# Attention with scores made twice: maxima first, then keys by queries, with the division on the output

## The chip, the cores and the metric

The kernel runs on one core of one Trainium2 chip. A core has TensorE (PE, matmuls into PSUM; weight loads are shown as PEld), VectorE (DVE), ScalarE (ACT), GpSimd (POOL) and SyncE (SP, which here only issues DMAs). They run in parallel, each through its own instructions in order, and wait for one another by semaphores. PSUM is 8 banks of 2 KB per partition, a bank holding 512 float32 of each of 128 partitions. The metric is the device time of one execution in microseconds (us).

## The reference

Eight batches of 12 heads, 448 tokens and 64 elements per head go through attention, whose output is laid out as 768 features per token, and then through a gated MLP whose gate mixes tokens.

```python
q_n, k_n = rmsnorm(q, g_q), rmsnorm(k, g_k)       # over a head's 64 elements
scores = 1 / sqrt(64) * q_n @ k_n.T
attn = exp(scores - max(scores, axis=-1))
attn = attn / (sum(attn, axis=-1) + 1e-9)
x = (attn @ v) -> (batch, 448, 768)
h = gelu(x @ w_in)                                # 768 -> 1024, tanh form
u, v = h[..., :512], h[..., 512:]
v_n = (v - mean(v)) / sqrt(var(v) + 1e-6) * g_ln
v_s = w_sg @ v_n + b_sg                           # over the 448 tokens
out = x + (u * v_s) @ w_out
```

## The kernel before

Float32 values are carried as two float16 parts, high and low, and a product is made of two or three matmuls of such parts. Heads go in pairs (A, B): 48 pairs, six per batch. 448 tokens are three blocks of 128 and a tail of 64; a pair is seven columns of 128 rows, the tails of A and B sharing one.

Per pair `i` the work runs through these functions. `squares` and `norms` (lines 317 to 339) make the root mean squares of q and k, for two pairs at a time: a square on ACT, a sum on DVE, some ten short operations on DVE. `split` (line 341) multiplies by gains and norms on POOL, makes the high part on ACT and the low part on POOL, copies the keys' parts in swapped order on DVE, and turns all with one DMA transpose into `qt` (line 352). `vsplit` (line 377) makes the parts `vh` and `vl` of v.

`scores` (line 395) has a tile of 128 queries by 448 keys per step, seven per pair. Each is two matmuls that contract over 128 rows (a head's 64 elements, high and low; line 411), or, for the tile of the tails, two for each head on half of the output partitions. DVE takes the row maximum from PSUM (line 414), ACT the exponential with that as bias and with the row sums (line 416). For groups of two, two and three tiles DVE makes the reciprocal of the sums (lines 420 and 422). The weights are then scaled into a high part (on POOL for some tiles, line 430, on ACT for the others, line 432) and a low part (DVE, line 433). As queries lie on the partitions and `pv` needs keys there, DMA transposes on SP's queue (line 436, four per pair) turn both parts into `at`.

`pv` (line 442) has 11 steps per pair; in each, both heads' matmuls (384 and 64 columns, lines 453 and 455) write their half of the output partitions of one PSUM tile. ACT and DVE make the parts `xh` and `xl` of x (lines 461 and 462), which stay in SBUF.

`moe` (line 485) is the MLP of a batch: `mv` (line 517 and 520, v's half of `x @ w_in`), gelus in a `cluster` on ACT with a load of the gelu table before and of the exponential's table behind it (lines 471 and 480), the layer norm, `mu` (line 575, u's half), `ms` (line 605, mixing tokens; the last 64 tokens' contraction is on half of the rows), the gate, and `mo` (lines 639 to 651, the output with x added through an identity), whose outputs leave by ACT's DMA queue (lines 658 to 661).

Weights are read and decoded in the first pairs (`weights`, line 153). The order is set at three places. Line 709 loops over the pairs and, per pair, interleaves the steps of `scores(i)`, `pv(i - 1)`, the weights and the MLP of an earlier batch by their counts of steps; `low` (line 668) puts the MLP's instructions 200 places later in priority; and a planner lays every engine's instructions out by priority and by when it expects their operands. What it lays out is fixed: on the chip each engine goes through its list in order. PSUM: `ps_s` has four one-bank buffers for the scores, `ps_v` one for pv, `ps_m` three for everything of the MLP (lines 84 to 86).

Of the kernel before, what the change touches and what calls it, by code (L numbers as in the profile page):

```python
# [8 lines left out]
F32 = mybir.dt.float32  # L9
# [24 lines left out]
PT, PT0 = (0, 3, 6), (0, 2, 4, 6)
# buffers
NS, NV, NM = 4, 1, 3
NQK, NVR, GV, RAWB = 2, 2, 3, 3
NA, NAH, NAT, NQT, NVH, HLB = 4, 4, 2, 2, 2, 2
NOT, NX = 2, 12
BACC_KW = dict(dynamic_dma_scratch_size=1024)  # L40
# [4 lines left out]
def kernel(  # L45
# [16 lines left out]
    P = 128  # L62
# [11 lines left out]
    C7 = 2 * CM + 1  # L74
    EH = DM // 2
# [34 lines left out]
    def newton(y, x, t):  # L110
        """y, a guess of x ** -0.5 within 3.5%, made better by a step of third and one of second order."""
        V.tensor_tensor(out=t, in0=x, in1=y, op=ALU.mult)
        V.tensor_tensor(out=t, in0=t, in1=y, op=ALU.mult)
        V.scalar_tensor_tensor(out=t, in0=t, scalar=-10.0 / 3.0, in1=t, op0=ALU.add, op1=ALU.mult)
        V.scalar_tensor_tensor(out=y, in0=t, scalar=5.0, in1=y, op0=ALU.add, op1=ALU.mult)
        V.scalar_tensor_tensor(out=t, in0=x, scalar=-0.5 * 0.375 ** 3, in1=y, op0=ALU.mult, op1=ALU.mult)
# [36 lines left out]
    def weights():  # L153
        nonlocal mlp
        ctx_w = ExitStack()
        # w_in's parts take the place of its float32 values, one K block after the other
# [60 lines left out]
        for c in range(CK):  # L217
# [15 lines left out]
        for j in range(2 * FT):  # L233
# [25 lines left out]
    R = {}  # L259

    def load_qk(i, qs=None):
        if i >= NI:
            return
        qs = qs or [nc.scalar]
        nq = 0

        def put(out, in_):
            nonlocal nq
            qs[nq % len(qs)].dma_start(out=out, in_=in_)
            nq += 1  # L270

        b, g = divmod(i, NP)
        h0 = 2 * g
        qk = ld.tile([P, 2, 2 * C7, D], F32, name="qk", bufs=NQK)
        def mains(j):
            for x, src in enumerate((q, k)):
                d = qk[:, j, x * C7:(x + 1) * C7]
                put(bass.AP(tensor=d.tensor, offset=d.offset, ap=[list(d.ap[0]), [CK * D, 2], [1, CM * D]]),
                    src[b, h0 + 2 * j:h0 + 2 * j + 2, 0:SM].rearrange("h (p c) d -> p h (c d)", c=CM))
            R[i + j] = dict(qk=qk[:, j])  # L280

        mains(0)
        for x, src in enumerate((q, k)):
            for h in range(2):
                put(qk[h * HP:(h + 1) * HP, :, x * C7 + CM],
                    src[b, h0:h0 + 4, SM:S].rearrange("(j h) p d -> h p j d", h=2)[h])
        mains(1)
# [3 lines left out]
    def load_v(i):  # L291
        """A head's v in 7 columns: m0, m1, m2, (t, m0a), (m0b, m1a), (m1b, m2a), (m2b, t), with a and b
        the halves of a block: what meets the blocks of A's transposed weights and, from (t, m0a) on, of B's."""
        if i >= NI:
            return
        b, g = divmod(i, NP)
        vr = ld.tile([P, 2 * GV, C7, D], F32, name="vr", bufs=NVR)
        hs = slice(2 * g, 2 * (g + GV))
        mn = v[b, hs, 0:SM].rearrange("h (p c) d -> p h (c d)", c=CM)
        tl = v[b, hs, SM:S].rearrange("h p d -> p h d")  # L300
        lo, hi = vr[0:HP], vr[HP:P]
        for dst, src in ((vr[:, :, 0:3].rearrange("p h c d -> p h (c d)"), mn),
                         (hi[:, :, 3:6].rearrange("p h c d -> p h (c d)"), mn[0:HP]),
                         (lo[:, :, 4:7].rearrange("p h c d -> p h (c d)"), mn[HP:P]),
                         (lo[:, :, 3], tl),
                         (hi[:, :, 6], tl)):
            nc.sync.dma_start(out=dst, in_=src)
        for j in range(GV):
            VR[i + j] = vr[:, 2 * j:2 * j + 2].rearrange("p h c d -> p (h c d)")

    def v8(x):
        """Of a pair's columns A's 0..3 and B's 3..6."""
        return bass.AP(tensor=x.tensor, offset=x.offset, ap=[list(x.ap[0]), [10 * D, 2], [1, 4 * D]])
# [3 lines left out]
    def squares(i):  # L317
        gi, j = divmod(i, NG)
        if j == 0:
            SS[gi] = sml.tile([P, NG, SSW], F32, name="ss", bufs=2)  # L320
        qk = R[i]["qk"]
        sk = prep.tile([P, 896], F32, name="sqk", tag="t4", bufs=HLB)
        skv = sk[:, 0:SSW * D].rearrange("p (c d) -> p c d", d=D)
        A.activation(out=skv, in_=qk, func=AF.Square)  # L324
        V.tensor_reduce(out=SS[gi][:, j], in_=skv, axis=AX.X, op=ALU.add)  # L325

    def norms(i, cnt):
        gi, j = divmod(i, NG)
        n = cnt * SSW
        ss = SS[gi].rearrange("p a b -> p (a b)")[:, j * SSW:j * SSW + n]  # L330
        x, t = (sml.tile([P, NG * SSW], F32, name=f"n{c}", bufs=2)[:, 0:n] for c in "xt")
        si = sml.tile([P, NG * SSW], I32, name="ni", bufs=2)[:, 0:n]
        yt = sml.tile([P, NG * SSW], F32, name="ny", bufs=3)
        y = yf = yt[:, 0:n]
        V.tensor_scalar(out=x, in0=ss, scalar1=1.0 / D, scalar2=1e-6, op0=ALU.mult, op1=ALU.add)
        rsqrt_guess(yf, si, x)
        newton(yf, x, t)
        for j in range(cnt):
            R[i + j]["rs"] = y[:, j * SSW:(j + 1) * SSW]

    def split(i, E=G):
        r = R[i]
        qk = r["qk"]
        E.tensor_tensor(out=qk[:, C7:], in0=qk[:, C7:], in1=gg.unsqueeze(1).broadcast_to([P, C7, D]), op=ALU.mult)  # L344
        E.tensor_tensor(out=qk, in0=qk, in1=r["rs"].unsqueeze(2).broadcast_to([P, SSW, D]), op=ALU.mult)  # L345
        hl = prep.tile([P, 3 * C7, 2, D], F16, name="hl", tag="t4", bufs=HLB)
        A.activation(out=hl[:, 0:SSW, 0], in_=qk, func=AF.Copy)  # L347
        E.tensor_tensor(out=hl[:, 0:SSW, 1], in0=qk, in1=hl[:, 0:SSW, 0], op=ALU.subtract)  # L348
# [8 lines left out]
    def vsquares(i):  # L357
        """The sums of squares of the GV pairs of heads from i on."""
        if i >= NI:
            return  # L360
# [435 lines left out]
```

## Time and profile before

| | |
|---|---|
| median of 3 runs | 1049.37 us (1048.88 to 1051.4) |
| span of the profiled execution | 1047.2 us |
| its mean granted TensorE clock | 0.903 |
| busy: PE, DVE, ACT, POOL | 809.6, 899.9, 705.4, 504.6 us |
| DMA transposes of the weights | 192 |

The profiled execution was not timed apart from its profile, so its time is its span; the median of the runs is 2.2 us above it. Busy time is that of an engine's own work: waiting, and issuing DMAs, do not count. A matmul's recorded length has its passage through the array, so successive matmuls overlap in the record, and the distance between two starts is what one costs. In a row of a group, `x336 | 289.6, 886` means 336 instructions, 289.6 us busy in all, 886 ns as the mean of one; behind the second bar stands the engine's idle time just before them and what ended it.

### The profile page before, as it was taken

Reading aid. Unit: us, or ns where it says so; the run is one execution under the profiler, and the core shown is the slowest. Engines: PE = TensorE matmul, PEld = TensorE weight load, DVE = VectorE, ACT = ScalarE, POOL = GpSimd, SP = SyncE. Lnnn points to the kernel's source line nnn. Section 1 sums busy time; section 2 is a strip of 40 time slices with the busy share of each in tenths; the row PEclk is TensorE's granted clock in tenths of the full one; section 3 lists DMA queues with packets and bytes.
Section 4 is the critical chain, followed back from the end, with each engine's and each line's share of the span. In section 5 each row is a group of like instructions: output and inputs, shape, how many; then the busy total and the mean of one; then the engine's idle time right before and its main releaser. Section 6 shows DMA issues by size and latency. Waiting matters only on the chain. (4 is left out here: it accounts for less than half of the span.)

```text
span 1047.2 us, 17092 instructions
## 1 busy us (share of the span) xinstructions
PE 809.6 (77%) x5652; PEld 447.3 (43%) x5652; DVE 899.9 (86%) x1959; ACT 705.4 (67%) x1418; POOL 504.6 (48%) x435
## 2 busy tenths in 40 slices
PE   0333556757689798888979899887979799799998
PEld 0111222424454346444644357343634365346546
DVE  4999979999789997999979998999889988999430
ACT  2565787676677777677767767587667686877441
POOL 1777745637536463443545372545455443535021
PEclk9666688888899899899999899999989999999999
DMA  5969589685989979996797879994989779838501
GB/s 144 254 174 244 125 179 215 160 185 108 207 180 206 194 156 206 173 217 152 162 213 181 167 149 196 202 211 106 207 190 195 148 166 201 180 89 174 110 1 61
DMA packets 528217, 177.74 MB, mean 170 GB/s; under 512 B 472257, under 2 KB 521985, under 8 KB 528129
## 3 DMA queue, kind: packets, MB, share of 16 engines
q1 hardware_dynamic: 484928, 144.07, 66.6%
q10 hardware_dynamic: 43200, 32.59, 11.3%
q8 instruction: 44, 0.72, 0.3%
q14 instruction: 45, 0.36, 0.1%
HBM read 54.58 MB, written 11.01 MB: 63 GB/s over the span
## 5 line engine op out<-in xcount | busy, mean ns | idle before, releaser
L433 DVE SCALAR_TENSOR_TENSOR ahl<-a,rc,ahl 128x448 f16<-128x448 f32 x336 | 289.6, 886 | 32.1 <-POOL ahl L430 22.0
L416 ACT ACTIVATE a<-s,nm 128x448 f32<-128x448 f32 x336 | 211.0, 630 | 124.7 <-DVE ahl L433 78.0
L411 PE MATMUL s<-qt 128*128 128x448 f16 (+1 forms) x768 | 192.2, 388 | 120.8 <-ACT a L416 63.5
L430 POOL TENSOR_SCALAR ahl<-a,rc 128x448 f16<-128x448 f32 x150 | 117.3, 786 | 230.0 <-DVE rc L422 99.9
L414 DVE TENSOR_REDUCE nm<-s 128x1 f32<-128x448 f32 x336 | 200.2, 610 | 18.5 <-PE s L411 18.0
L432 ACT ACTIVATE ahl<-a,rc 128x448 f16<-128x448 f32 x186 | 118.1, 662 | 61.5 <-DVE rc L422 34.2
L411 PEld LDWEIGHTS <-qt 128*128 128x128 f16 (+1 forms) x768 | 57.2, 105 | 209.2 <-issue 127.8
L345 POOL TENSOR_TENSOR qk<-qk,ny 128x896 f32<-128x896 f32 x47 | 83.2, 1792 | 70.6 <-DVE ny L118 34.4
L348 POOL TENSOR_TENSOR hl<-qk,hl 128x896 f16<-128x896 f32 x47 | 95.7, 2037 | 34.4 <-ACT hl L347 26.3
L453 PE MATMUL pv<-at,vl 128*64 128x384 f16 x384 | 68.2, 368 | 56.7 <-DMA at<-ahl 44.8
L344 POOL TENSOR_TENSOR qk<-qk,gg 128x448 f32<-128x448 f32 x47 | 58.9, 1255 | 77.0 <-ACT sqk L324 76.8
L453 PE MATMUL pv<-at,vh 128*64 128x384 f16 x672 | 91.0, 357 | 0.0
L575 PEld LDWEIGHTS <-wi 128*128 128x128 f16 x576 | 57.4, 102 | 61.8 <-issue 15.9
L455 PE MATMUL pv<-at,vh 128*64 128x64 f16 x672 | 78.7, 202 | 0.0
L611 POOL TENSOR_TENSOR gt<-gt,u 128x448 f32<-128x448 f32 x32 | 39.0, 1221 | 79.0 <-DVE gt L610 59.2
L453 PEld LDWEIGHTS <-vl 128*64 128x64 f16 x384 | 30.7, 118 | 90.0 <-DMA at<-ahl 37.0
L416 ACT ACTIVATION_READ_ACCUMULATOR a<-s,nm 128x1 f32 x336 | 65.9, 196 | 0.0
L325 DVE TENSOR_REDUCE ss<-sqk 128x14 f32<-128x896 f32 x48 | 51.5, 1073 | 15.5 <-ACT sqk L324 15.2
L347 ACT ACTIVATE hl<-qk 128x896 f16<-128x896 f32 x48 | 45.3, 945 | 25.6 <-DMA qk<-in_k_dram 11.4
L324 ACT ACTIVATE sqk<-qk 128x896 f32<-128x896 f32 x48 | 45.3, 944 | 21.7 <-DVE ss L325 11.2
L453 PEld LDWEIGHTS <-vh 128*64 128x64 f16 x672 | 50.2, 120 | 18.6 <-issue 0.8
L420 DVE TENSOR_SCALAR rc<-sums 128x2 f32<-128x2 f32 x144 | 52.1, 364 | 7.1 <-ACT a L416 6.5
(995 smaller groups left out, 2096.0 us busy)
## 6 DMA issues: line engine op xcount, KB each, us to landing
qk<-in_k_dram ACTq DMA_DIRECT2D x48, 192.0 KB, 3.6
vr<-in_v_dram SPq DMA_DIRECT2D x16, 576.0 KB, 4.9
vr<-in_v_dram SPq DMA_DIRECT2D x32, 288.0 KB, 5.9
out_dram<-ot ACTq DMA_DIRECT2D x24, 384.0 KB, 3.8
qk<-in_q_dram ACTq DMA_DIRECT2D x46, 192.0 KB, 3.6
raw<-in_moe_w_in_dram SPq DMA_DIRECT2D x12, 512.0 KB, 4.9
vr<-in_v_dram SPq DMA_DIRECT2D x32, 96.0 KB, 4.9
at<-ahl SPq DMA_TRANSPOSE x192, 3.8
```

What stands on the lines that cost most here:

```text
L344: E.tensor_tensor(out=qk[:, C7:], in0=qk[:, C7:], in1=gg.unsqueeze(1).broadcast_to([P, C7, D]), op=ALU.mult)
L345: E.tensor_tensor(out=qk, in0=qk, in1=r["rs"].unsqueeze(2).broadcast_to([P, SSW, D]), op=ALU.mult)
L348: E.tensor_tensor(out=hl[:, 0:SSW, 1], in0=qk, in1=hl[:, 0:SSW, 0], op=ALU.subtract)
L411: mm(out=ps[p0:p1], lhsT=qt[:, t * P + p0:t * P + p1], rhs=qt[:, k0:k0 + S], start=(n == 0), stop=(n == 1))
L414: V.tensor_reduce(out=nm, in_=ps, axis=AX.X, op=ALU.max, negate=True)
L416: A.activation(out=a, in_=ps, func=AF.Exp, bias=nm, accum_out=sums[:, t - t0:t - t0 + 1])
L430: G.tensor_scalar(out=hl[:, 0], in0=a, scalar1=sc, scalar2=1.0, op0=ALU.mult, op1=ALU.mult)
L432: A.activation(out=hl[:, 0], in_=a, func=AF.Copy, scale=sc)
L433: V.scalar_tensor_tensor(out=hl[:, 1], in0=a, scalar=sc, in1=hl[:, 0], op0=ALU.mult, op1=ALU.subtract)
L453: mm(out=o[:, 0:SM].rearrange("p (c n) -> p c n", c=CM), lhsT=w, rhs=at[:, h * CK:h * CK + CM, blk], start=(n == 0), stop=(n == n_s - 1), ...
L455: mm(out=o[:, SM:S], lhsT=w, rhs=at[:, CM, blk, h * HP:(h + 1) * HP], start=False, stop=(n == n_s - 1), skip_group_check=True)
L575: done = mm(out=ps[:, 0:S], lhsT=ww[:, g, f * P:(f + 1) * P], rhs=xx, start=(n == 0), stop=(n == 17))
```

## The change

The scores are made twice and the weights come out with keys on the partitions, as `pv` needs them. `maxima(i)` multiplies the high parts alone, queries on the partitions, and takes each query's maximum. The negated maxima, as float16, are turned into a row (a matmul of the maxima against an identity) and copied to SBUF with ln 256 added; what is subtracted need not be the exact maximum, since the division takes it out again. `scores(i)` has keys on the partitions: three products of parts and a fourth that adds the row, then exponential, high part and low part. `pv(i)` first sums the weights over the keys by matmuls with ones, ACT makes the reciprocal as exp(-ln(sum)), one step of Newton corrects it, and the output is multiplied by it. The 192 transposes and `rc` are gone.

Each head keeps to one half of TensorE's rows: `qt` holds head A's 64 elements on partitions 0 to 63 and B's on 64 to 127, in four parts (q high, q low, k high, k low), for two pairs at a time, made by two transposes of 14 columns. PSUM is shared out anew: `ps_s` two buffers of two banks (for maxima, row and scores), `ps_v` one each for sums and pv, `ps_m` two. Token `7 p + c` now goes to block `c`, in 64 rows, so that loads, outputs, `w_sg` and `b_sg` are cut in seven; q and k are loaded on SP's queue, eight DMAs per two pairs, v once per batch without repeated columns, and outputs leave on SP's queue, two DMAs per tile. The MLP is as before, but at the two early batches two tiles of `mv` in place of three run along with the heads, and which results of `mv` and `mu` are copied out of PSUM ahead of their gelu is changed. The activation table set that holds exponential and logarithm is loaded in place of the exponential's.

```diff
-NS, NV, NM = 4, 1, 3
+SC, SR, SV = 4, 5, 5          # steps per pair: scores, maxima, pv
+EX = 256.0
+NS, NV, NM = 2, 1, 2
...
     def split(u, E=G):
+        qt = att.tile([P, 4, C7 * P], F16, name="qt", bufs=NQT)
+        for x in range(2):
+            qk = r["qk"][:, x].rearrange("p h c d -> p (h c) d")
+            if x:
+                E.tensor_tensor(out=qk, in0=qk, in1=gg..., op=ALU.mult)
+            E.tensor_tensor(out=qk, in0=qk, in1=r["rs"]..., op=ALU.mult)
+            A.activation(out=h_, in_=r["qk"][:, x], func=AF.Copy)
+            E.tensor_tensor(out=l_, in0=r["qk"][:, x], in1=h_, op=ALU.subtract)
+            r["tr"] = nc.sync.dma_start_transpose(out=qt[:, 2 * x:2 * x + 2]..., in_=hl...)
...
+    def bank(t, n, h):
+        return t[:, h, 0:S] if n == P else t[h * HP:(h + 1) * HP, 0, 0:S]
+
+    def maxima(i):
+        for c, (c0, n) in enumerate(tiles):
+            ps = ps_s.tile([P, 2, 512], F32, name="mx", tag="s")
+            for h in range(2):
+                hs = slice(h * HP, (h + 1) * HP)
+                mm(out=bank(ps, n, h), lhsT=qt[hs, 0, c0:c0 + n], rhs=qt[hs, 2, cols], start=True, stop=True)
+            V.tensor_reduce(out=nm[:, 2 * c:2 * c + 2], in_=ps[:, :, 0:S], axis=AX.X, op=ALU.max, negate=True)
+            yield
+        ps = ps_s.tile([P, 2, 512], F32, name="row", tag="s")
...
+                mm(out=ps[hs, 0, o:o + n], lhsT=nm[ks, x:x + 1].broadcast_to([n, HP]), rhs=ident_h[ks, ks], ...)
+        A.activation(out=row, in_=ps[:, 0, 0:S], func=AF.Copy, bias=LN_EX)
+
     def scores(i):
+        for c, (c0, n) in enumerate(tiles):
+            ps = ps_s.tile([P, 2, 512], F32, name="s", tag="s")
+            for m, (kx, qx) in enumerate(((2, 0), (2, 1), (3, 0), (None, None))):
+                for h in range(2):
+                    if m < 3:
+                        mm(out=bank(ps, n, h), lhsT=qt[hs, kx, c0:c0 + n], rhs=qt[hs, qx, cols], start=(m == 0), stop=False)
+                    else:
+                        mm(out=bank(ps, n, h), lhsT=part_h[hs, 0:n], rhs=row[hs], start=False, stop=True)
+            A.activation(out=p_, in_=p_, func=AF.Exp)
+            A.activation(out=h_, in_=p_, func=AF.Copy)
+            V.tensor_tensor(out=l_, in0=p_, in1=h_, op=ALU.subtract)
+            yield
-                nm = sml.tile([P, 1], F32, name="nm", bufs=6)
-                V.tensor_reduce(out=nm, in_=ps, axis=AX.X, op=ALU.max, negate=True)
-                A.activation(out=a, in_=ps, func=AF.Exp, bias=nm, accum_out=sums[:, t - t0:t - t0 + 1])
-            V.tensor_scalar(out=rc[:, 0:n], in0=sums[:, 0:n], scalar1=1.0 / ASC, scalar2=1e-9 / ASC, ...)
-            V.reciprocal(out=rc[:, 0:n], in_=rc[:, 0:n])
-                    G.tensor_scalar(out=hl[:, 0], in0=a, scalar1=sc, scalar2=1.0, op0=ALU.mult, op1=ALU.mult)
-                    A.activation(out=hl[:, 0], in_=a, func=AF.Copy, scale=sc)
-                V.scalar_tensor_tensor(out=hl[:, 1], in0=a, scalar=sc, in1=hl[:, 0], op0=ALU.mult, op1=ALU.subtract)
-                    nc.sync.dma_start_transpose(out=at[:, first:t + 1]..., in_=ahl[:, 0:cnt]...)
...
     def pv(i):
+        steps = [[(x, slice(0, P), c + h * C4, 2 * c + h) if c < CM else (x, slice(h * HP, (h + 1) * HP), CM, 2 * CM)
+                  for h in range(2)] for c in range(C4) for x in range(2)]
+        sm = ps_v.tile([P, 512], F32, name="sm")[:, 0:S]
+        for n, hx in enumerate(steps):
+            for h, (x, ks, _, t) in enumerate(hx):
+                mm(out=sm[h * HP:(h + 1) * HP], lhsT=one_h[ks], rhs=(ph, pl)[x][ks, t], ...)
+        A.activation(out=ln, in_=sm, func=AF.Ln)
+        A.activation(out=rc, in_=ln, func=AF.Exp, scale=-1.0)
+        ps = ps_v.tile([P, 512], F32, name="pv")[:, 0:S]
+        for vx, px in ((vh, ph), (vl, ph), (vh, pl)):
+            for hx in steps[::2]:
+                for h, (_, ks, c, t) in enumerate(hx):
+                    mm(out=ps[h * HP:(h + 1) * HP], lhsT=vx[ks, c], rhs=px[ks, t], ...)
+            yield
+        V.scalar_tensor_tensor(out=sm, in0=sm, scalar=1e-9 * EX, in1=rc, op0=ALU.add, op1=ALU.mult)
+        V.tensor_tensor(out=y, in0=ps, in1=rc, op=ALU.mult)
+        V.scalar_tensor_tensor(out=ps, in0=sm, scalar=-2.0, in1=y, op0=ALU.add, op1=ALU.mult)
...
-                nc.scalar.dma_start(out=om[t], in_=ot)
+            for h in range(2):
+                nc.sync.dma_start(out=om[1][t + h * C4] if t < CM else om[h][CM], in_=ot[h * HP:(h + 1) * HP])
...
         streams = []
         if i < NI:
-            streams.append((scores(i), 14))
+            streams.append((scores(i), SC))
+        if i + 1 < NI:
+            streams.append((maxima(i + 1), SR))
         if i > 0:
-            streams.append((pv(i - 1), 4))
+            streams.append((pv(i - 1), SV))
```

More of the change, by code (lines that the diff above doesn't have):

```diff
@@ L96 @@
     make_identity(nc, ident)
+    ident_h = const.tile([P, P], F16, name="ident_h")
+    A.activation(out=ident_h, in_=ident, func=AF.Copy)
+    one_h = const.tile([P, HP], F16, name="one_h")
+    V.tensor_copy(out=one_h, in_=ones[:, 0:HP])
+    part_h = const.tile([P, P], F16, name="part_h")
+    V.tensor_scalar(out=part_h, in0=ones, scalar1=1.0 / HP, scalar2=None, op0=ALU.mult)
     swap = const.tile([P, P], F32, name="swap")
@@ L263, in load_qk @@
+    lo, hi = slice(0, HP), slice(HP, P)
+    def load_qk(u, qs=None):
+        if u >= NI // NG:
             return
-        qs = qs or [nc.scalar]
+        qs = qs or [nc.sync]
         nq = 0
[L267 to L280, printed above, removed]
@@ L282, in load_qk @@
-        mains(0)
-        for x, src in enumerate((q, k)):
[L284 to L287, printed above, removed]
+        b, h0 = u // NU, u % NU * 2 * NG
+        qk = ld.tile([P, 2, 2, C7, D], F32, name="qk", bufs=NQK)
+        for x, src in enumerate((q, k)):
+            for half, j, b0, c0, n in ((lo, 0, 0, 0, C4), (hi, 0, 0, C4, CM), (lo, 1, C4, C4, CM), (hi, 1, CM, 0, C4)):
+                qs[nq % len(qs)].dma_start(
+                    out=qk[half, x, :, b0:b0 + n].rearrange("p h c d -> p h (c d)"),
+                    in_=src[b, h0 + 2 * j:h0 + 2 * j + 2].rearrange("h (p c) d -> p h (c d)", c=C7)[:, :, c0 * D:(c0 + n) * D])
+                nq += 1
@@ L289, with load_v @@
+        U[u] = dict(qk=qk)
     VR = {}
-    def load_v(i):
-        if i >= NI:
+    def load_v(b):
+        if b >= B:
             return
[L296 to L309, printed above, removed]
@@ new lines, in load_v @@
+        for j, h, half, s0, c0, n in ((0, 0, lo, 0, 0, C4), (0, 0, hi, 0, C4, CM), (0, 1, lo, C4, 0, CM), (0, 1, hi, CM, CM, C4),
+                                      (1, 0, lo, 0, C4, CM), (1, 0, lo, CM, 0, 1), (1, 0, hi, 0, 1, CM),
+                                      (1, 1, lo, C4, C4, CM), (1, 1, hi, CM, 0, C4)):
+            nc.sync.dma_start(out=vp[half, :, j, s0 * D:(s0 + n) * D], in_=src[j, h][:, :, c0 * D:(c0 + n) * D])
+        for g in range(NP):
+            VR[b * NP + g] = vr[:, g].rearrange("p c d -> p (c d)")
@@ L322, in squares @@
+    SS = {}
+    def squares(u, x):
+        if x == 0:
+            SS[u] = sml.tile([P, 2, SSW], F32, name="ss", bufs=2)
         sk = prep.tile([P, 896], F32, name="sqk", tag="t4", bufs=HLB)
         skv = sk[:, 0:SSW * D].rearrange("p (c d) -> p c d", d=D)
[L324 to L334, printed above, removed]
-        V.tensor_scalar(out=x, in0=ss, scalar1=1.0 / D, scalar2=1e-6, op0=ALU.mult, op1=ALU.add)
[L336 to L339, printed above, removed]
@@ new lines, in squares, with norms @@
+        V.tensor_reduce(out=SS[u][:, x], in_=skv, axis=AX.X, op=ALU.add)
+    def norms(u):
+        n = 2 * SSW
+        ss = SS[u].rearrange("p a b -> p (a b)")
+        x, t = (sml.tile([P, n], F32, name=f"n{c}", bufs=2) for c in "xt")
+        si = sml.tile([P, n], I32, name="ni", bufs=2)
+        y = sml.tile([P, n], F32, name="ny", bufs=3)
+        V.tensor_scalar(out=x, in0=ss, scalar1=1.0 / D, scalar2=1e-6, op0=ALU.mult, op1=ALU.add)
+        rsqrt_guess(y, si, x)
+        newton(y, x, t)
+        U[u]["rs"] = y
@@ new lines, in pv @@
+        ln, rc, y = (att.tile([P, S], F32, name=x, bufs=1) for x in ("ln", "rc", "y"))
+        A.activation(out=ln, in_=sm, func=AF.Ln)
+        A.activation(out=rc, in_=ln, func=AF.Exp, scale=-1.0)
+        yield
+        ps = ps_v.tile([P, 512], F32, name="pv")[:, 0:S]
+        n = 0
+        for vx, px in ((vh, ph), (vl, ph), (vh, pl)):
+            for hx in steps[::2]:
+                for h, (_, ks, c, t) in enumerate(hx):
+                    mm(out=ps[h * HP:(h + 1) * HP], lhsT=vx[ks, c], rhs=px[ks, t], start=(n == 0), stop=(n == 3 * C4 - 1),
+                       skip_group_check=True)
+                n += 1
+            yield
```

268 lines of the change are left out of this document (117 added, 151 removed).

## The prediction

> **What bounds the kernel now.** I read the page's busy line and slices first, then the table of stretches, then the groups of instructions kept apart by shape, then the timeline of TensorE. The page:
>
> ```profile
> span 1047.2 us, 17092 instructions
> PE 809.6 (77%) x5652; PEld 447.3 (43%) x5652; DVE 899.9 (86%) x1959; ACT 705.4 (67%) x1418; POOL 504.6 (48%) x435
> PEclk9666688888899899899999899999989999999999
> ```
>
> The stretches (span; PE, PEld, DVE, ACT, POOL busy with counts; granted clock, DMA share, GB/s) show a start, a long even middle and a drain. The second fence is the same view for line 461 alone (ACT's first output copy, one per pair of heads), so its count is the number of pairs finished; the third is line 411 (the scores' matmuls), the fourth the tile pv (PE, DVE, ACT).
>
> ```profile
> 0.00:250.00 250.00, 123.59 (x734) 56.30 (x734) 223.57 (x469) 158.58 (x311) 145.62 (x116) 0.77 0.78 179
> 250.00:985.00 735.00, 631.00 (x4552) 355.63 (x4553) 663.97 (x1455) 524.52 (x1074) 348.94 (x308) 0.94 0.84 179
> 985.00:1047.20 62.20, 55.02 (x369) 35.33 (x367) 12.34 (x36) 22.33 (x34) 10.07 (x12) 0.99 0.08 26
> ```
> ```profile
> 250.00:985.00 735.00, 21.33 (x40) 0.94 0.84 179
> ```
> ```profile
> 250.00:985.00 735.00, 148.38 (x614) 43.80 (x614) 0.94 0.84 179
> ```
> ```profile
> 250.00:985.00 735.00, 111.94 (x1720) 24.40 (x40) 21.33 (x40) 0.94 0.84 179
> ```
>
> In the middle 40 pairs take 735 us: 18.4 us per pair. DVE is busy 664.0/40 = 16.6 us of each (90%), PE 15.8, ACT 13.1. Of PE's 15.8, scores are 148.4/40 = 3.7, pv 2.8, and the MLP the remaining 9.3. In the start DVE is busy 89%. So **DVE sets the pace** in both, with PE at 86% behind it; only the drain is PE's. The question is whether PE has 2.6 us per pair to spare for what the change adds.
>
> **DVE, ACT, POOL and DMA, per pair** (group busy time over 48 pairs). What they spend now:
>
> ```profile
> L433 DVE SCALAR_TENSOR_TENSOR ahl<-a,rc,ahl 128x448 f16<-128x448 f32 x336 | 289.6, 886 | 32.1 <-POOL ahl L430 22.0 <-ACT ahl L432 10.1
> L416 ACT ACTIVATE a<-s,nm 128x448 f32<-128x448 f32 x336 | 211.0, 630 | 124.7 <-DVE ahl L433 78.0 <-DVE nm L414 32.4 <-DVE rc L420 4.1
> L414 DVE TENSOR_REDUCE nm<-s 128x1 f32<-128x448 f32 x336 | 200.2, 610 | 18.5 <-PE s L411 18.0
> L432 ACT ACTIVATE ahl<-a,rc 128x448 f16<-128x448 f32 x186 | 118.1, 662 | 61.5 <-DVE rc L422 34.2 <-issue 11.4 <-DVE nt L116 2.6
> L430 POOL TENSOR_SCALAR ahl<-a,rc 128x448 f16<-128x448 f32 x150 | 117.3, 786 | 230.0 <-DVE rc L422 99.9 <-ACT a L416 28.3 <-DVE rc L420 16.6
> L416 ACT ACTIVATION_READ_ACCUMULATOR a<-s,nm 128x1 f32 x336 | 65.9, 196 | 0.0
> L325 DVE TENSOR_REDUCE ss<-sqk 128x14 f32<-128x896 f32 x48 | 51.5, 1073 | 15.5 <-ACT sqk L324 15.2
> L384 ACT ACTIVATE vh<-vr,v_s 128x896 f16<-128x896 f32 x48 | 49.6, 1035 | 6.8 <-DVE v_s L134 3.8 <-DMA at<-ahl 2.9
> L386 DVE SCALAR_TENSOR_TENSOR vl<-vr,v_s,vh 128x512 f16<-128x512 f32 x48 | 47.3, 986 | 0.1
> L347 ACT ACTIVATE hl<-qk 128x896 f16<-128x896 f32 x48 | 45.3, 945 | 25.6 <-DMA qk<-in_k_dram 11.4 <-DVE ss L325 5.3 <-DMA qt<-hl 4.5
> L420 DVE TENSOR_SCALAR rc<-sums 128x2 f32<-128x2 f32 x96 | 32.5, 343 | 1.3 <-ACT a L416 1.1
> L462 DVE SCALAR_TENSOR_TENSOR xl<-pv,xh 128x448 f16<-128x448 f32 x48 | 29.3, 610 | 9.5 <-ACT xh L461 9.5
> L461 ACT ACTIVATE xh<-pv 128x448 f16<-128x448 f32 x48 | 25.6, 533 | 18.0 <-PE pv L455 17.7 <-PE s L411 0.2
> L351 DVE COPY hl<-hl 128x448 f16<-128x448 f16 x48 | 25.4, 531 | 0.1
> ```
>
> - DVE loses the low parts (289.6/48 = 6.03), the seven maxima (4.17), the row scales of the first two groups (0.68; the smaller reciprocals are left out) and a copy of key halves (0.53): 11.4 us, with the 0.99 of vl. It gets maxima on 896 wide tiles (3 at line 325's 1.07, also 896 wide, and one at 0.61: 3.8), low parts `l_` (3 + 1 of the same sizes; line 462, which reads PSUM and one SBUF tile likewise, took 0.61 for half: 3.8 to 4.3, I take 4.0), three operations of the division at 0.61 (1.8), and vl of 448 (0.99 x 448/512 = 0.87). That is 10.5 against 12.4: 1.9 off for certain; the reciprocals and the other copy add perhaps 1. I take **3 us** with them and without the slowing of line 433 (0.89 for what line 462 does in 0.61). DVE comes to 13.6 to 14.7 per pair.
> - ACT loses (211.0 + 65.9 + 118.1 + 49.6)/48 = 9.3 and gets exp and the high copy of 896 (6 at 0.945, from line 347) and of the tail (2 at 0.53, from line 461), the row 0.53, logarithm and exponential of the sums 2 x 0.63 (line 416), vh 0.53: 9.0. No change.
> - POOL loses 117.3/48 = 2.4 and is nowhere near the pace.
>
> ```profile
> at<-ahl SPq DMA_TRANSPOSE x192, 3.8
> qk<-in_k_dram ACTq DMA_DIRECT2D x48, 192.0 KB, 3.6
> ```
>
> - The 192 transposes of the weights leave SP's queue, and with them a landing of 3.8 us between scores and pv. The q, k loads (ACT's queue until now) and the outputs come to SP: 8 loads per two pairs, two outputs per MLP tile, 9 loads of v per batch. A load waits for its qk buffer, with the transposes of later keys behind it; it is issued two units (some 37 us) ahead, against a landing of 3.6. Cost nothing; if that cover were gone, 3.6 us in each of 24 units, 86 us.
>
> **TensorE.** Its timeline (start, length, instruction, count) gives the price of a matmul as the distance of starts:
>
> ```profile
> 600.23 0.35 PE L605 MATMUL ms__6887<-ws_l,vh 128*128 128x448 f16 x1
> 600.42 0.35 PE L605 MATMUL ms__6804<-ws_h,vl 128*128 128x448 f16 x1
> 600.71 0.36 PE L605 MATMUL ms__6804<-ws_h,vh 64*128 64x448 f16 x1
> ...
> 602.26 0.36 PE L605 MATMUL ms__6887<-ws_h,vh 64*128 64x448 f16 x1
> 602.26 0.36 PE L605 MATMUL ms__6804<-ws_h,vl 64*128 64x448 f16 x1
> 602.46 0.35 PE L605 MATMUL ms__6887<-ws_l,vh 64*128 64x448 f16 x1
> 602.47 0.35 PE L605 MATMUL ms__6832<-ws_h,vl 64*128 64x448 f16 x1
> ```
> ```profile
> 604.59 0.34 PE L453 MATMUL pv<-at,vh 128*64 128x384 f16 x2
> 604.75 0.20 PE L455 MATMUL pv<-at,vh 128*64 128x64 f16 x2
> 604.78 0.34 PE L453 MATMUL pv<-at,vh 128*64 128x384 f16 x2
> ```
>
> Three things are to be seen. A matmul of 448 columns takes 0.19 us of PE (600.23 to 600.42). Two on different halves of the rows start together (602.26 twice, 602.46 and 602.47), and so do two heads on halves of the columns (x2, with 0.19 from 604.59 to 604.78): a slot of 0.19 holds two heads. And when the shape of the array changes, the next start is 0.29 later, not 0.19 (600.42 to 600.71): **0.1 us per change of shape**.
>
> Slots per pair now: scores 6 tiles x 2 and the tail 2, 14; pv 11. 25 x 0.19 = 4.75 us (busy is 6.5: a lower clock, ends, changes of shape). After: maxima 4, scores 4 tiles x 4 (three products and the row), sums 8, pv 12: 40 x 0.19 = 7.6, and four short ones for the row, 128 columns, 4 x 0.19 x 128/448 = 0.2. So 7.8, and with the MLP's 9.3 **PE needs 17.1 us per pair before any change of shape**.
>
> Changes of shape: today full tiles of the scores have the MLP's shape, 128 by 128. After the change nothing of attention has: maxima and scores are 64 by 128, sums and pv 128 by 64, tails 64 by 64. Nine pieces per pair (4 maxima, row, 4 scores) take the two PSUM buffers one by one as these come free, between MLP matmuls: in and out, 18. The sums and pv run in 4 groups, each with a tail step, some 7 more. At least 12, if pieces stay together; at most 33, if each is alone. I take 25, nearer the upper end, because the buffers come free singly: 2.5 us (bounds 1.2 and 3.3). PE then needs 19.6 (18.3 to 20.4).
>
> How full PE can be is bounded by DVE's 90% in the middle and by this stretch, where PE has 53.97 of 60 (90%), at a full clock, just before the attention ends:
>
> ```profile
> 900.00:960.00 60.00, 53.97 (x381) 28.85 (x380) 57.44 (x126) 45.56 (x92) 30.84 (x28) 1.00 0.60 129
> ```
>
> A PE that sets the pace gets the full clock, which gives back up to 6% of its columns (0.94 in the middle) against these 90%; I take 96% net. 19.6/0.96 = 20.4 us per pair.
>
> **New waits.** The scores' fourth product needs the row, a copy on ACT behind the four maxima on DVE; the next pair's maxima run beside this pair's scores, so a pair's time (18 us) covers it, and only the first pair pays. The division hangs on sums, logarithm, exponential and three operations on DVE, with one PSUM buffer each for sums and pv: 1.5 + 2 x 0.63 + 3 x 0.61 + 0.53 + 0.61 = 5.7 us, within one pair's time too. PE's next sums wait behind it, and MLP matmuls behind these, only if it more than doubles. Nothing is added.
>
> **The sum.** Middle: 40 x (20.4 - 18.4) = +80. Start: 8 pairs in which DVE sets the pace and PE is busy 123.6 of 250: 3 us each, -24; the first keys and queries are now split for two pairs before any score, on DVE, three operations of 896 more at 1.07, +3: -21. Drain: with two PSUM buffers for the MLP in place of three, only two tiles of v are summed ahead; the third, 18 matmuls of 512 columns (0.19 x 512/448 = 0.22 each), moves behind the last head: +4, and 1 for waits: +5 (0 to 10). The profiled execution spans 1047.2 and the median of the runs is 1049.4, so 2.2 lie around it: 1047.2 + 80 - 21 + 5 + 2.2 = **1113**. PE from 18.3/0.98 = 18.7 to 20.4/0.90 = 22.7 gives 1045 to 1205; a start that gains 24 to 30, and the shapes below 12, reach lower.
>
> **Rivals.**
> - *Changes of shape are few, and it gets faster.* With 9 per pair (0.9 us) PE needs 18.0, at 98% 18.4: the middle keeps its time, and the start's gain stands: 1047.2 - 21 + 5 + 2.2 = 1033. Equality is at 18.8 us per pair, which at 98% is 13 changes of shape. For it: line 411's matmuls ran in fours between others. Against: only two PSUM buffers for nine pieces.
> - *The two PSUM buffers of the scores set the pace.* A full scores tile holds one through 4 slots of two matmuls' time (0.76), exp and copy (0.945 each) and the low part (1.07), 3.7 us; the tail 2.4, a maximum 1.3 (0.8 for the tail's), the row 0.8: 3 x 3.7 + 2.4 + 3 x 1.3 + 0.8 + 0.8 = 19.0 us, 9.5 per pair over two buffers. Every handing over, 17 of them, may meet another operation of up to 1 us on ACT or DVE. Half a wait of 1.5 us leaves it harmless, the whole 1.5 makes (19.0 + 25.5)/2 = 22.3: 1033 + 40 x 3.9 = 1189. For it, waits of this kind today, with four buffers (us, times, longest):
>
> ```profile
> ACT a L416 <- DVE ahl L433: 78.0, 80, 4.7
> PE s L411 <- ACT a L416: 63.5, 40, 7.9
> ```
>
> - *The tails of the two heads do not run together.* They lie in the two halves of one PSUM bank and on different halves of the rows, where the pairs at 602.26 wrote two tiles. Then the tails' 10 slots (maxima 1, scores 4, sums 2, pv 3) double: 1.9 us per pair, at 96% 2.0 x 40 = 80: 1193. The Trainium skill says of row halves that different row tiles cannot access the same PSUM bank at the same time (TensorEngine Tiling (Array Packing), Gotcha 1: PSUM Pressure); no run here shows such a pair yet. By that rule the time would be this rival's, by the row at 602.26 the forecast's.
> - *The halves don't overlap at all.* 20 more slots, 3.8 us, +158 at 96%: 1271. Against: the rows at 602.26.
>
> **Chances.** PE sets the pace at some 20.4 us: 0.46. Few changes of shape: 0.22. PSUM buffers: 0.15. Tails one after the other: 0.14. No overlap: 0.03. About 0.3% (3 us) is what can be told from no change. Within 3 us I count 0.03 of the first case (its fast edge) and 0.01 of the second: slower 0.43 + 0.15 + 0.14 + 0.03 = 0.75, no change 0.04, faster 0.21. The range, 1026 to 1190, leaves out the fastest of the second case, half of the two cases near 1190, and the last; the likeliest alone has 1075 to 1150 (19.4 to 21.3 us per pair).
>
> **What would show it.** After: DVE down to 75% or less of the middle with PE at 90% or more and the clock near 1.0; maxima and scores in pairs of equal start 0.19 apart; 0.1 more where shapes change. Tails: two starts together or 0.19 apart. Waits of PE for ACT or DVE at the scores above 2 us per pair would make it the buffers. A PE below 85% with less time would make the forecast wrong in kind, a middle below 18.8 us per pair in sign.

## The result and the profile after

The changed kernel takes 1292.96 us (median of 4 runs, 1291.99 to 1293.67) against 1050.38 us before on the same chip: a ratio of 1.2318, with a 95% interval of 1.226 to 1.2376. Slower was forecast, but 1113 us, and the time lies far above the range of 1026 to 1190. The profiled execution spans 1291.1 us. Below, a time without an interval behind its ratio is that of a single run.

The page of the changed kernel:

```profile
span 1291.1 us, 18006 instructions
PE 1056.3 (82%) x6996; PEld 479.4 (37%) x6996; DVE 781.4 (61%) x1430; ACT 727.3 (56%) x1095; POOL 347.7 (27%) x259
PEclk9666779999888997999888998999789899999899
```

The same stretches as before, cut where 7, 40 and 1 pairs of heads are finished, as they were there (columns: span; PE, PEld, DVE, ACT, POOL busy with counts; clock, DMA share, GB/s), and below it the count of the pairs, line 475 being ACT's first output copy:

```profile
0.00:260.00 260.00, 152.00 (x902) 57.59 (x904) 194.73 (x361) 156.74 (x243) 106.55 (x78) 0.79 0.40 104
260.00:1225.00 965.00, 849.90 (x5760) 387.10 (x5758) 574.25 (x1034) 548.28 (x818) 231.07 (x170) 0.93 0.23 52
1225.00:1291.10 66.10, 54.38 (x338) 34.66 (x338) 12.38 (x36) 22.32 (x34) 10.05 (x12) 0.97 0.10 25
```
```profile
0.00:260.00 260.00, 3.76 (x7) 0.79 0.40 104
260.00:1225.00 965.00, 21.71 (x40) 0.93 0.23 52
```

By this cut a pair takes 965/40 = 24.1 us in the middle, 18.4 before and 20.4 in the forecast. DVE has fallen to 14.4 us of it (60%), PE risen to 21.2 (88%). So PE is the busiest by far, and yet it stands still for 2.9 us per pair, and the clock is 0.93 and not full.

The cut at 260 us falls inside a long eighth pair, whose output copy starts at 278.6 us (at 250.4 before). Whole pairs compare better: from the eighth output copy to the 48th (1225.0 and 987.2 us) a pair takes 23.7 us, and 18.4 before. So the miss of 180 us is the middle's 40 x (23.7 - 20.4) = 130, and the start's 49: it takes 28 us more than before where 21 less were forecast. The drain behind the 48th copy (66 us against 60) is as forecast.

Who PE and the others waited for (us in all, times, longest):

```profile
PE s L431 <- DVE nm L401: 104.4, 42, 8.3
PE mx L399 <- DVE pl L438: 24.8, 18, 5.4
PE mx L399 <- DVE nm L401: 15.9, 8, 5.8
DVE pl L438 <- ACT ph L437: 142.5, 70, 5.6
DVE nm L401 <- PE mx L399: 127.5, 58, 4.3
DVE ss L316 <- ACT sqk L315: 60.3, 23, 5.7
ACT s L436 <- PE s L433: 159.2, 87, 5.8
ACT hl L341 <- DMA qt<-hl: 38.0, 15, 4.2
```

PE waits for DVE at maxima and scores (145 us in these three rows), DVE for ACT at the low parts, ACT for PE at the scores: a ring in which each stands idle for the next. What they share are the two PSUM buffers, which maxima and scores take in turn: line 431 does not read the maxima, so its wait for one is for the buffer that the maximum frees. One stretch shows a second thing in that ring (PE, DVE and ACT; start, length, and in brackets the idle time before):

```profile
497.83 0.68 PE L465 MATMUL pv<-pl,vh 128*64 128x448 f16 x3
502.11 0.55 PE L399 MATMUL mx<-qt 64*128 64x448 f16 x2 [3.60 <-DVE nm L401]
507.27 1.31 PE L431 MATMUL s<-qt 64*128 64x448 f16 x6 [4.61 <-DVE nm L401]
```
```profile
493.95 0.62 DVE L438 TENSOR_TENSOR pl<-s,ph 128x448 f16<-128x448 f32 x1 [0.45 <-ACT ph L437]
499.98 1.09 DVE L316 TENSOR_REDUCE ss<-sqk 128x14 f32<-128x896 f32 x1 [5.40 <-ACT sqk L315]
500.98 1.08 DVE L401 TENSOR_REDUCE nm<-mx 128x2 f16<-128x896 f32 x1
```
```profile
497.02 0.95 ACT L341 ACTIVATE hl<-qk 128x896 f16<-128x896 f32 x1 [2.38 <-DMA qt<-hl]
498.99 0.95 ACT L315 ACTIVATE sqk<-qk 128x896 f32<-128x896 f32 x1 [1.02 <-DMA qt<-hl]
```

ACT waits for a transpose of keys to give back a staging buffer, DVE's sum of squares waits 5.4 us for ACT, a maximum stands behind that sum in DVE's queue, and PE waits for the maximum. The ring and this chain are both waits for buffers. The theories, told in the expectations as they were formed before the runs: A, the keys' staging buffers; B, the scores' two PSUM buffers; C, PE's own work.

### The profile page after: what moved, and what is told of

Its sections match the earlier page's. It is cut to its first block, busy times and chain, and to the rows that moved or that the text cites. A ratio compares the mean times of both kernels' runs of the same rounds, so it can differ in the third digit from the quotient of the medians.

```text
span 1291.1 us, 18006 instructions
## 1 busy us (share of the span) xinstructions
PE 1056.3 (82%) x6996; PEld 479.4 (37%) x6996; DVE 781.4 (61%) x1430; ACT 727.3 (56%) x1095; POOL 347.7 (27%) x259
## 4 chain that ended last, share of the span: by engine, by line
PE 57%; DVE 17%; DMA 8%; ACT 7%; issue 5%; POOL 3%; SPq 2%; POOLq 0%; DVEq 0%; ACTq 0%
PE pv L465 7%; PE s L431 7%; PE sm L452 6%; DMA qt<-hl 5%; DVE nm L401 3%; DVE pl L438 3%; PE mx L399 2%; PE s L433 2%; DVE ss L316 2%; POOL qk L337 1%; SPq L285 1%; DVE sm L470 1%; DVE y L471 1%; ACT s L436 1%; ACT sqk L315 1%
## 5 line engine op out<-in xcount | busy, mean ns | idle before, releaser
L438 DVE TENSOR_TENSOR pl<-s,ph 128x896 f16<-128x896 f32 x192 | 186.2, 970 | 144.1 <-ACT ph L437 142.5
L431 PE MATMUL s<-qt 64*128 64x448 f16 (+1 forms) x1152 | 163.3, 388 | 113.6 <-DVE nm L401 104.4
L436 ACT ACTIVATE s<-s 128x896 f32<-128x896 f32 x192 | 155.5, 810 | 177.9 <-PE s L433 159.2
L401 DVE TENSOR_REDUCE nm<-mx 128x2 f16<-128x896 f32 x144 | 156.3, 1085 | 127.5 <-PE mx L399 127.5
L437 ACT ACTIVATE ph<-s 128x896 f16<-128x896 f32 x192 | 157.0, 819 | 2.6
L399 PE MATMUL mx<-qt 64*128 64x448 f16 (+1 forms) x384 | 78.2, 400 | 68.6 <-DVE pl L438 24.8
L431 PEld LDWEIGHTS <-qt 64*128 64x128 f16 (+1 forms) x1152 | 54.1, 101 | 194.2 <-issue 176.7
L452 PE MATMUL sm<-ph,one_h 128*64 128x448 f16 (+1 forms) x384 | 82.3, 422 | 18.3 <-DVE pv L472 7.9
L452 PE MATMUL sm<-pl,one_h 128*64 128x448 f16 (+1 forms) x384 | 79.1, 402 | 0.0
L433 PE MATMUL s<-row,part_h 64*128 64x448 f16 (+1 forms) x384 | 77.9, 388 | 0.0
L399 PEld LDWEIGHTS <-qt 64*128 64x128 f16 (+1 forms) x384 | 24.0, 99 | 131.5 <-issue 107.2
```

The lines of the kernel that those rows point to most:

```text
L399: mm(out=bank(ps, n, h), lhsT=qt[hs, 0, c0:c0 + n], rhs=qt[hs, 2, cols], start=True, stop=True)
L401: V.tensor_reduce(out=nm[:, 2 * c:2 * c + 2], in_=ps[:, :, 0:S], axis=AX.X, op=ALU.max, negate=True)
L431: mm(out=bank(ps, n, h), lhsT=qt[hs, kx, c0:c0 + n], rhs=qt[hs, qx, cols], start=(m == 0), stop=False)
L433: mm(out=bank(ps, n, h), lhsT=part_h[hs, 0:n], rhs=row[hs], start=False, stop=True)
L436: A.activation(out=p_, in_=p_, func=AF.Exp)
L437: A.activation(out=h_, in_=p_, func=AF.Copy)
```

## The experiments

**A third buffer for the transposed keys.**

```diff
-NPT, NQT, NVH, HLB = 2, 2, 2, 3
+NPT, NQT, NVH, HLB = 2, 3, 2, 3
```

> Three buffers for the transposed queries and keys (qt) in place of two; all else as in the changed kernel. Three theories of the changed kernel's 24.1 us per pair. Theory A, the keys' buffers: the transposes of split wait on SP for a qt buffer, so the t4 buffers that they read stay held, ACT's square and copy of the next unit wait for one (52 us in the profile), and DVE's in-order queue stands behind the sum of those squares (60 us) with the maxima behind it. Then a third qt buffer takes away 60 to 115 us: 1180 to 1235, and DVE's wait for ACT at the sums of squares falls below 20 us. Theory B, the two PSUM buffers of the scores: within 1%, 1280 to 1305. Theory C, PE's own work at 88% is all there is: within 1%.

1282.0 us, a ratio to before of 1.2213 (1.2181 to 1.2244): 11 us less, and DVE's wait at the sums of squares is 54.8 us still. The wait is there, but a third qt buffer is not what ends it, and as far as the qt buffers go, A accounts for little of the miss. A further staging buffer was not tried.

**Scores leave PSUM sooner.**

```diff
-            A.activation(out=p_, in_=p_, func=AF.Exp)
-            A.activation(out=h_, in_=p_, func=AF.Copy)
-            V.tensor_tensor(out=l_, in0=p_, in1=h_, op=ALU.subtract)
+            a = att.tile([P, 2, S], F32, name="a", bufs=3)[:, 0:w]
+            A.activation(out=a, in_=p_, func=AF.Exp)
+            A.activation(out=h_, in_=a, func=AF.Copy)
+            V.tensor_tensor(out=l_, in0=a, in1=h_, op=ALU.subtract)
```

> The exponential writes float32 to SBUF (three buffers) in place of its own PSUM tile, and the high copy and the low part read it there, so a scores tile leaves PSUM after one ACT operation and not after two and one of DVE. PE's work is the same. Theory B (two PSUM buffers of the scores): the hold of a tile falls from 3.7 to about 1.9 us, PE's waits for DVE at the scores and maxima (130 us in the profile) fall by half or more: 60 to 115 us less, 1180 to 1235. Theory A (the keys' buffers): the stalls of DVE's and ACT's queues stay, within 1.5%, 1274 to 1310. Theory C (PE's work): within 1%.

1183.39 us, a ratio of 1.1267 (1.1228 to 1.1305): 110 us less, as B said. Its middle, 40 pairs by the count of the second fence:

```profile
275.00:1117.00 842.00, 814.15 (x5669) 379.18 (x5667) 570.59 (x1000) 536.46 (x798) 231.85 (x158) 0.99 0.25 56
```
```profile
275.00:1117.00 842.00, 21.53 (x40) 0.99 0.25 56
```

This is the state that the forecast described: PE busy 814.15 of 842 (97%) at a clock of 0.99, a pair every 21.05 us. These are the pairs from the eighth copy on, so the stretch to set beside it is the 23.7 us of the changed kernel: 2.6 us per pair, 104 of the 110 us. PE has the same matmuls, DVE's low part is slower (1.22 us in place of 1.09), and the order that the planner gives is no better in changes of shape (28.9 per pair against 26.1), so what the edit saves is the hold of the two PSUM buffers. PE's longest waits for them are left with these:

```profile
PE mx L399 <- DVE nm L401: 27.1, 16, 8.4
PE s L431 <- ACT a L437: 23.7, 12, 4.7
```

The wait of DVE at the sums of squares falls to 33.7 us too, without a buffer more for the keys: part of it came from the ring.

**Attention without the MLP.** The MLP's body is replaced by a copy of one pair's values and zeros to the output; weights are still read.

```diff
     def moe(b, early=False):
-        ...
+            G.memset(ot[:, S:DM], 0.0)
+            A.activation(out=ot[:, 0:S], in_=XT[b * NP][0], func=AF.Copy)
```

> Leaves out the MLP but for the reading of its weights (each batch writes one head pair's values and zeros to the output): attention alone. Theory C: PE has 10.3 to 13.8 us per pair, DVE 12, ACT 11, so a pair takes 14 to 15 us, in all some 720 to 800. Theory B: the buffers' hold with queueing stays near 20 us per pair, in all 950 to 1100. Theory A: a stall of some 5 us per two pairs on top of 14: 16.5 per pair, 800 to 880.

1067.76 us. PE has lost the MLP's 9 us per pair, and the time is still above that of the whole kernel before (1048.35 us on this chip). The middle of it (500 us, and ACT's output copies in it), and what PE waits for:

```profile
300.00:800.00 500.00, 321.39 (x2110) 114.87 (x2109) 303.01 (x487) 269.04 (x389) 115.87 (x74) 0.74 0.29 66
```
```profile
300.00:800.00 500.00, 12.93 (x24) 0.74 0.29 66
```
```profile
PE s L431 <- DVE nm L401: 152.7, 69, 7.8
PE mx L399 <- DVE nm L401: 82.1, 19, 7.8
```

500/24 = 20.8 us per pair (19.7 from the eighth output copy to the 48th), with PE, DVE and ACT busy 64, 61 and 54%. None of them sets that pace alone; the time is in the range of B.

**The same with three PSUM buffers.** Without the MLP its banks are free.

```diff
-NS, NV, NM = 2, 1, 2
+NS, NV, NM = 3, 1, 0
```

> As e_noml (attention alone, 1068 us), with three PSUM buffers of two banks for maxima, row and scores in place of two (the MLP's banks are free there). Theory B (these buffers set the pace): 19.9 us per pair fall towards two thirds, 14 to 16, the time to 800 to 880. If the pace is that of the chain of engines within a pair, or of the keys' buffers (theory A): above 1020.

901.94 us, 22 us beyond what B gave; 30 output copies in the same 500 us, 16.7 us per pair, 0.80 of the 20.8 where buffers alone would give two thirds. One buffer more takes a fifth off every pair, and with it something else comes near.

**The kernel before, without its MLP.** The same edit there.

> The kernel before without the MLP, left out as in e_noml: attention alone, with its four one-bank PSUM buffers and the transposes. If DVE sets its pace (16.6 us per pair, of it some 2 the MLP's and weights'), a pair takes 15.5 to 17 us, and the whole 820 to 900, against 1068 for the changed kernel's attention alone. If the pace before hung on buffers or landings too: 930 to 1000.

880.45 us, inside the expectation for a pace set by DVE, which is busy 89% of it. Its attention alone is faster than the changed one by 187 us.

**Without maxima.**

```diff
     def maxima(i):
-        ...
+        r["row"] = row_c
+        yield
```

> Leaves out the maxima and the row of them (a constant of 11.5 is subtracted from all scores instead): per pair 8 maxima matmuls, 8 short ones, some 10 changes of shape, 4 maxima on DVE, the row's copy on ACT and 5 of the 9 uses of the scores' PSUM buffers fall away. Theory C: PE loses 0.76 + 0.4 + 1.0 = 2.2 of its 21.3 busy us per pair, at the same 88% 2.5 x 48: 1293 - 120 = 1173 (1155 to 1195). Theory B: the uses of the buffers fall from 19 to 13.5 us of hold and 5 of 17 hand-overs go, so the 2.8 us idle go as well: 1293 - 48 x 5 = 1050 (1030 to 1100). Theory A: the maxima no longer stand in DVE's queue behind the sums of squares, but the low parts do: 1120 to 1180.

1119.68 us, a ratio of 1.0667 (1.0621 to 1.0712). That is 173 us less, more than C's 120 and less than B's 243, so neither as it was put. Of it, 70 us are gone by the eighth output copy (209 us in place of 279), and from there to the 48th a pair takes 20.5 us; the drain is longer. Between 300 and 1000 us it finishes 34 pairs, 20.6 us each, with PE busy 99%:

```profile
300.00:1000.00 700.00, 693.55 (x4324) 312.39 (x4323) 369.97 (x759) 444.00 (x657) 187.03 (x131) 0.98 0.24 58
```

PE sets this pace, and needs nearly as much per pair as in the kernel with maxima. Why, the run "Early release and no maxima" below tells.

**Both buffers.** Scores out of PSUM early (two buffers for `a`), and the third buffer for the keys.

```diff
-NPT, NQT, NVH, HLB = 2, 2, 2, 3
+NPT, NQT, NVH, HLB = 2, 3, 2, 3
+            a = att.tile([P, 2, S], F32, name="a", bufs=2)[:, 0:w]
+        y = ln
```

> e_early with two SBUF buffers for the exponentials, and e_nqt3's third qt buffer (the reciprocal's y takes the place of ln, for room). Theory B with PE behind it (in e_early PE is busy 96% of the middle at a full clock): what the third qt buffer gave alone, 11 us, is mostly hidden now, 1170 to 1190. If theory A has been hidden behind B: 1130 to 1160.

1168.87 us, 1.1124 (1.1086 to 1.1162), 14.5 less than with the early release alone and just beyond what was expected with PE behind B. It is the fastest version that does all of the changed kernel's work, and 11% slower than before.

**Fewer changes of shape.** In sums and pv the tails' steps contract over all rows, so that the array keeps its shape there; the output is then not attention's.

```diff
-            ... if c < CM else (x, slice(h * HP, (h + 1) * HP), CM, 2 * CM)
+            ... if c < CM else (x, slice(0, P), CM, 2 * CM)
```

> e_early, and in sums and pv the tails' steps contract over all 128 rows, both heads' tails mixed (the output is then not attention's; the work is a pure change of shape): sums and pv keep one shape of the array, 7 changes of shape of 0.1 us per pair fewer. If PE sets e_early's pace: 0.7 x 48 = 34 us less, 1140 to 1160. If the buffers still do: within 10 us of e_early, 1173 to 1193.

1159.8 us, 1.104 (1.1001 to 1.1079): 23.6 less. Counted in the trace, between 300 and 1050 us, changes of shape fell from 28.9 to 23.8 per pair, by 5.1 and not 7, and 5.1 x 0.1 x 48 = 24. That the two agree is luck: 19 of the 23.6 us are gained before the eighth output copy (252.3 us in place of 271.6), where PE is busy some 63%. From there to the 48th PE's busy time falls from 20.4 to 19.9 us per pair, which is the price of the changes, but the pair only from 21.1 to 20.9, and PE waits for the rest. So PE's pace is one bound of the early version, and another lies close behind it.

**Half of the sums.**

```diff
+        hs_ = steps[::2]
-        for n, hx in enumerate(steps):
+        for n, hx in enumerate(hs_):
```

> e_early without the low parts in the sums (left out: 4 of 8 steps of the sums, a relative change of about a two-thousandth): 4 slots of 0.21 and 2 changes of shape fewer per pair, nothing else. If PE sets e_early's pace: 1.0 x 48 = 48 us less, 1125 to 1150. If not: within 10 us, 1173 to 1193.

1150.15 us, 1.0938 (1.0909 to 1.0967): 33 less of the 48. Between the eighth and the 48th output copy PE's busy time falls by the 1.0 us per pair that was expected, and the pair by 0.65: again PE's work sets the pace only in part.

**Early release and no maxima.**

> e_early and e_nomax together (the maxima and their row left out, a constant in their place): nothing of the scores' buffers is left to wait for, and PE has 2.2 us per pair less than in e_early. If e_nomax (1120 us, PE busy 89% of all) was PE's pace already: within 15 us of it, 1100 to 1120. If the buffers still cost it something: below 1090.

1166.94 us, where 1100 to 1120 or less was expected: 47 us more than without maxima alone, with the same matmuls. PE is busy 98% in it too. Its timeline shows what for:

```profile
602.28 0.39 PE L512 MATMUL mv__5572<-wi,xh 128*128 128x512 f16 x1
602.60 0.36 PE L410 MATMUL s<-qt 64*128 64x448 f16 x1
602.89 0.39 PE L512 MATMUL mv__5572<-wi,xh 128*128 128x512 f16 x1
603.21 0.36 PE L410 MATMUL s<-qt 64*128 64x448 f16 x1
603.50 0.60 PE L512 MATMUL mv__5612<-wi,xh 128*128 128x512 f16 x2
```

The planner has laid the MLP's and the scores' matmuls alternately, one by one. A scores matmul then has no partner on the other half of the rows; it takes the place of both, and the shape changes on either side of it. From 602.28 to 603.50, 1.22 us pass for two MLP matmuls (0.22 each) and two such halves, each of which would take 0.1 beside its partner: 0.63. Counted in the trace between 300 and 1000 us, such lone halves are some 2.0 per pair of heads in the changed kernel, 3.5 in the early version, 9.8 without maxima and 13.1 here; the changes of shape, 26.1 (260 to 1225 us), 28.9 (300 to 1050), 31.2 and 36.6.

**The same, with the MLP further back in priority.**

```diff
-MOFF, MOFF0, GP = 200, 100, 350
+MOFF, MOFF0, GP = 2000, 2000, 350
```

> e_early_nomax (1167 us), with the MLP's instructions 2000 places later in priority in place of 100 and 200, so that the planner lays attention's matmuls in longer runs: in its list PE changes between attention's and the MLP's matmuls, or between attention's kinds, 436 times in place of 1304, and 32 runs in place of 490 end with one head's matmul alone. Theory C with the order (PE sets the pace; every change of shape costs 0.1 us and a matmul alone costs half a slot more): 87 + 44 us less, 1036 (1020 to 1080). If e_early_nomax is slower than e_nomax for the SBUF copies' sake (DVE's low part 1.25 us in place of 1.09, contention): within 20 us of 1167.

1082.32 us, 1.0322 (1.0255 to 1.039): 85 us less than the same matmuls in the other order. 1.4 lone halves and 16.4 changes of shape per pair are left; PE is busy 93% of 300 to 1000 us, so some of the 131 us expected went to waits. So the order cost these 85 us. With the maxima left in, the same edit was not run, and what the order costs there is open.

**Copies off DVE in the kernel before**, to test that DVE sets its pace.

```diff
-        V.tensor_copy(out=hl[:, SSW:, 0], in_=hl[:, C7:SSW, 1])
-        V.tensor_copy(out=hl[:, SSW:, 1], in_=hl[:, C7:SSW, 0])
+        G.tensor_copy(out=hl[:, SSW:, 0], in_=hl[:, C7:SSW, 1])
+        G.tensor_copy(out=hl[:, SSW:, 1], in_=hl[:, C7:SSW, 0])
```

> The kernel before with the two copies of key halves (lines 350 and 351, 0.85 us of DVE per pair) on GpSimd in place of DVE. If DVE sets the pace before, as the prediction says: DVE is relieved by 41 us in all, the time falls by 15 to 40 us, to 1010 to 1035. If GpSimd's part in split (three operations of 1.3 to 2.0 us, now with two copies behind them) makes the keys late, or slows DVE's own SBUF operations more: 1045 to 1075.

1083.36 us, 1.032 (1.0287 to 1.0353): slower, and beyond both expectations. DVE has no less to do (the last row is line 112 before):

```profile
PE 822.4 (76%) x5652; PEld 447.7 (41%) x5652; DVE 902.7 (83%) x1863; ACT 706.8 (65%) x1420; POOL 562.5 (52%) x531
```
```profile
L351 POOL COPY hl<-hl 128x448 f16<-128x448 f16 x48 | 34.1, 709 | 16.2 <-ACT hl L347 16.2
L112 DVE TENSOR_TENSOR nt<-nx,ny 128x28 f32<-128x28 f32 x23 | 13.6, 590 | 0.2
```
```profile
L112 DVE TENSOR_TENSOR nt<-nx,ny 128x28 f32<-128x28 f32 x23 | 6.4, 279 | 0.2
```

41 us of copies are gone from DVE and its busy time is 902.7 against 899.9: other operations of it took longer. Line 112, of 28 elements, took 590 ns here and 279 before. So this edit could not test the claim. That DVE set the pace before rests on its 90% and on the kernel before without its MLP; no run that relieves DVE shows it.

## Why the prediction was wrong

**What bounded the kernel before: supported** by DVE's share and the run without the MLP.

**What DVE, ACT, POOL and the DMAs lose: held.** DVE was put at 13.6 to 14.7 us per pair and has 14.4; the low part of a full tile took 1.09 and the maximum 1.09 us, where 1.07 to 1.2 and 1.07 were taken. The loads on SP's queue do not appear among the waits of PE, DVE or ACT above.

**Slots and changes of shape: held.** Two heads run together, and the changes of shape are 26.1 per pair where 25 were taken. Six tail matmuls, with the MLP matmul ahead of them and what follows:

```profile
521.12 0.38 PE L532 MATMUL mv__4812<-wi,xh 128*128 128x512 f16 x1
521.43 0.75 PE L431 MATMUL s<-qt 64*64 64x448 f16 x6
522.02 0.35 PE L433 MATMUL s<-row,part_h 64*64 64x448 f16 x2
```

Six matmuls in 522.02 - 521.43 = 0.59 us, three slots of 0.2: the tails run together, and that rival falls. The rule named with it, that different row tiles cannot access the same PSUM bank at the same time (the Trainium skill, TensorEngine Tiling (Array Packing), Gotcha 1: PSUM Pressure), does not bind here, where the two write different partitions of the bank.

**PE's need per pair: mis-sized by 0.75 us.** 19.6 were forecast; in the early version it is busy 814.15/40 = 20.35. Lone halves were not in the sum at all: 3.5 per pair, each half a slot, 0.33; 3.9 changes of shape more there, 0.4. These two would make it up, but they are not the only ones: the middle one of the 128 by 64 slots takes 0.21 us there, where 0.19 was taken, so the other terms were not all right in size.

**How full PE would be: the step that failed.** "I take 96% net" was drawn from a stretch of the kernel before, with its four buffers. After the change PE was 88% busy at a clock of 0.93 and delivered 19.6/24.1 = 81% of the forecast's measure. The early version reached 97% at 0.99 with the same work, so it is the buffers that kept it at 88%, and the clock went with it. Of the middle's 130 us, the early release gives 104 back; the other 26 are about what PE's greater need and its last waits come to. That was a rival with a chance of 0.15, priced at 1189. Its hold was too short: 3.7 us for a full scores tile and 2.4 for the tail, 3.4 on the mean, are the operations end to end, and in the trace a scores tile holds its buffer for 5.3 us on the mean from its first matmul to the end of its low part, a maximum 2.1, the row 1.2. That is 15.0 us of each pair's 23.7 in each buffer, where the rival's sum had 9.5 before its hand-overs; in the early version it is 10.6. It also stood alone, as if PE's pace or the buffers' would set the time. Without the MLP the kernel with two buffers takes 19.7 us per pair; PE's work is 20.4; together they made 23.7. PE's list is in order, and what PE waits for at the scores it does not get back from the MLP behind: that fits these figures, but no run tests it apart.

**The start: wrong in sign.** -21 forecast, +28 measured at the eighth output copy. It was costed by DVE's relief, and DVE is busy 194.7 of 260 us in it, 75%: relieved, but no longer the pace. Without maxima the sixth pair's output copy starts at 157 us against 205 with them and 178 before, so much of what holds the start hangs on the maxima, which go through the same two buffers and through DVE's queue with the weights' decoding in it. Without the MLP a third buffer brings the sixth pair from 227 to 201 us, so it is not their number alone; and in the early version the edit of the tails alone brings the eighth copy forward by 19 us. Which part of the maxima it is, and what else, stays open.

**New waits: "nothing is added" was wrong.** The row itself is covered, as forecast: ahead of its matmuls (line 433) PE stands idle for 6.2 us in all, and never for another engine. What is added is the wait for the buffers: PE's largest wait is for DVE's maximum to free one, 104.4 us. The keys' staging buffers, at which DVE's queue stands 60 us, were not considered; a third qt buffer alone gave 11 us, and 14.5 in the early version.

**The drain: held,** 66 us against 60 behind the 48th output copy, +6 where +5 was taken.

**The other rivals.** Few changes of shape: they were 26.1. No overlap: the halves overlap.

## What to carry to other kernels

When work moves onto the engine that will be the bound, count its time per step and then ask separately how it will be fed: add up how long each PSUM buffer is held per step, with a wait at every hand-over, and compare that with the pace. Two bounds close to each other gave more than either here (19.7 and 20.4 us gave 23.7). A tile that goes through three operations on two engines in place should leave PSUM at the first of them; that one edit was worth 110 us here. Matmuls on halves of the array pay only when the partner stands next in the list, so look at the order that the planner gives, and move the filling work back in priority if it is laid between partners (85 us in the version without maxima).

## What the runs showed of the hardware

- Two matmuls on diagonal quarters of the array (different rows, different columns) that write the two halves of one PSUM bank run together: three such pairs in 0.59 us.
- A change of the array's shape costs 0.1 us also between 64 by 64 and the other shapes: an MLP matmul of 0.22 us is followed after 0.31 (521.12 to 521.43 us) where the shape changes to 64 by 64, and 5.1 changes fewer per pair took 0.47 us off PE's busy time per pair.
- The same matmuls took 85 us more when laid alternately with others (13.1 lone halves and 36.6 changes of shape per pair against 1.4 and 16.4).
- Copies moved from DVE to GpSimd took longer there (0.71 us against 0.53 for line 351), and DVE's busy time did not fall; a 28-element operation of DVE (line 112) went from 279 to 590 ns.
- The granted clock went with PE's busy share of a stretch: 0.74 at 64% (attention alone), 0.93 at 88% (the changed kernel), 0.99 at 97% (the early version).
